# Attention with one query, forward and backward: transposes as fp32 blocks, and sums in four column groups

## The chip, the core and the metric

The kernel runs on one core of a Trainium2 chip. A core has a matrix engine (TensorE, PE in the profile; its weight loads have a row of their own, PEld), a vector engine (VectorE, DVE), a scalar engine (ScalarE, ACT), GpSimd (POOL), and SyncE (SP), which here only issues transfers. 16 DMA engines move data between the main memory (HBM) and the core's memory (SBUF); TensorE writes to PSUM, which VectorE and ScalarE read. The metric is the device time in microseconds of one execution.

## The reference

For each of 64 heads (batch 2, 32 heads) there is one query row q of 128 elements, k and v of 8192 x 128, and a gradient g of 128 elements; all are bf16.

```python
scores = jnp.einsum("bhqd,bhkd->bhqk", q, k) * scale      # scale = 128 ** -0.5
p = softmax(scores)
out = jnp.einsum("bhqk,bhkd->bhqd", p, v)
_out, _vjp = jax.vjp(_f, q, k, v)
_grads = _vjp(grad_out)
return (_out, *_grads)
```

With dp = v g and dS = p (dp - sum(p dp)), the outputs are o = p v, dq = scale dS k, dk = scale dS q (an outer product of 8192 x 128) and dv = p g (another). Per head k and v are read (2 MB each) and dk and dv are written (2 MB each): 8 MB a head, 537 MB in all.

## The kernel before, in words

**Tiles.** k or v of one head is one SBUF tile of 128 partitions x 64 rows x 128 elements (2 MB); partition p holds rows 64p to 64p+63. There are 12 such tiles (NTILE), for six heads. dk and dv are made in place of k and v (`outer`, L427), stored from there, and the tile is loaded anew with k or v of the head six later (`load`, L100, with `slot_of`). Loads are issued by SP, stores by POOL (L445, or L89 in two parts); the last head's stores go in eight parts by SP. A load of a tile waits for the store of what lies in it. A head has four chunks (NCH) of 16 rows a partition (CH) for k and four for v.

**Split stores.** dk of the heads in SPREAD (4, 11, ..., 53: eight heads) is stored by `by_rows` (L89) as two transfers of 126 and of 2 partitions.

**One step.** The loop over g runs one chunk a step, eight steps a head; what later stages of earlier heads have to do is done in the same step. All instructions are kept in program order on each engine (`pin`). In a step PE does, in this order:

- `broadcast` (L178, in two of the steps): q or g of the head into all partitions, as a matmul of a broadcast column with the identity; VectorE copies it to qb (L187).
- `transpose_chunk` (L194): 16 transposes of 128x128 bf16 into the PSUM tile tp (two of these), which ScalarE copies to ev (L196, 128x2048, two of these).
- `join` (L409), the last sum over partitions of dq or o.
- `acc` (L372): four matmuls that sum 16 rows of a chunk of v (or k) by E_pad (or dS_pad). The weights are CW = 64 columns of the padded row of probabilities, the moving operand 512 columns; they go to NG = 2 groups of 64 output partitions. Of the 64 output rows in a group only four hold sums that are wanted; `pick` (L389, L395) takes them out with the mask `diag`.
- `spread_rows` (L228, in two of the steps): the scores lie in PSUM as rows (`raw`, copied to `rows` by VectorE, L221); four fp32 matmuls with the selector sel4 lay them over the partitions. An fp32 matmul is shown as two weight loads and two matmuls.
- `max_spread` (L251) and, on ScalarE, `expo` (L271); also `total` (L315) and, as an fp32 transpose, `max_all` (L244).
- `score_chunk` of the chunk before (L208): four matmuls over the 512 columns each of ev, into four groups of 32 output partitions. The weights are 32 columns of qdT that hold q (or g) in one column and zeros beside it; the chunk decides where the window on qdT begins, and so which row of `raw` the scores go to.

`outer` for head i comes in the steps 9 to 12 (dv) and 13 to 16 (dk) after the head's first. VectorE does `outer`, `pick`, the copies out of PSUM and the small steps of the softmax.

Of the kernel before, what the change touches and what calls it, by code (L numbers as in the profile page):

```python
# [9 lines left out]
ALU = mybir.AluOpType  # L10
AX = mybir.AxisListType
BF16 = mybir.dt.bfloat16
F32 = mybir.dt.float32

CH = 16
QT = 4
CW = 64
NG = 2
SG = 4
SW = 32  # L20
NTILE = 12
FIRST = 6
SPREAD = range(4, 60, 7)


@with_exitstack
def kernel(
# [11 lines left out]
    nc = tc.nc  # L39
    B, H, Sq, D = q.shape  # L40
    Sk = k.shape[2]
    P = nc.NUM_PARTITIONS
    assert Sq == 1 and D == P
    BH = B * H
# [3 lines left out]
    NCH = NT // CH  # L48
# [71 lines left out]
        load(j, 0)  # L120
        load(j, 1)

    ident_bf = const.tile([P, P], BF16)
    masks.make_identity(nc, ident_bf[:])
    ident_f = const.tile([P, P], F32)
    masks.make_identity(nc, ident_f[:])
    ones = const.tile([P, 1], F32)
    nc.vector.memset(ones[:], 1.0)
    groups = [g * P // NG for g in range(NG)]
# [8 lines left out]
    nc.vector.memset(E_pad[:], 0.0)  # L138
    nc.vector.memset(dS_pad[:], 0.0)

    sel4 = const.tile([P, NCH, SG], F32)
    nc.vector.memset(sel4[:], 0.0)
    for g in range(SG):
        nc.vector.tensor_copy(
            out=sel4[g * SW : (g + 1) * SW, :, g],
            in_=ident_f[g * SW : (g + 1) * SW, g * SW : g * SW + NCH],
        )

    Q0 = NCH - 1
    qdT = const.tile([P, 2, Q0 + NCH * BH + SW], BF16)  # L150
    nc.vector.memset(qdT[:], 0.0)
    for w in range(2):
        tps = ps_m.tile([P, BH], BF16, tag=f"acc{w}", name="tps")
        nc.tensor.transpose(tps[:], qd_nat[:BH, w, :], ident_bf[:BH, :BH])
        nc.vector.tensor_copy(
            out=qdT[:, w, Q0 : Q0 + NCH * BH].rearrange("p (i f) -> p i f", f=NCH)[:, :, 0],
            in_=tps[:],
        )

    dqT = const.tile([P, BH], BF16)  # L160
    oT = const.tile([P, BH], BF16)
# [1 line left out]
    def begin(i):  # L163
# [7 lines left out]
        h.lsum = sw[:, 2 * NT + 2 * P : 2 * NT + 2 * P + 2]  # L171
        h.mb = sw[:, 2 * NT + 2 * P + 2 : 2 * NT + 2 * P + 3]

    def broadcast(i, w):

        h = heads[i]
        pin(
            nc.tensor.matmul(  # L178
                h.qbp,
                lhsT=qdT[:, w, Q0 + NCH * i : Q0 + NCH * i + 1].to_broadcast([P, P]),  # L180
                rhs=ident_bf[:],
                start=True,
                stop=True,
            )
        )
        h.qb[w] = small.tile([P, D], BF16, tag=f"qb{w}", name="qb")
        pin(nc.vector.tensor_copy(out=h.qb[w][:], in_=h.qbp))  # L187

    def transpose_chunk(i, c):
        w, c = divmod(c, NCH)  # L190
        src = heads[i].tile[w]
        tp = ps_tp.tile([P, CH, P], BF16, tag="tp", name="tp")
        for t in range(CH):
            pin(nc.tensor.transpose(tp[:, t, :], src[:, c * CH + t, :], ident_bf[:]))  # L194
        ev = evp.tile([P, CH, P], BF16, tag="ev", name="ev")
        pin(nc.scalar.copy(out=ev[:], in_=tp[:]))  # L196
        return ev

    def score_chunk(i, c, ev):

        h = heads[i]
        w, c = divmod(c, NCH)
        if c == 0:
            h.raw = ps_sdp.tile([P, QT * P], F32, tag="raw", name="raw")
        q0 = Q0 + NCH * i - c
        for g in range(SG):
            pin(
                nc.tensor.matmul(  # L208
                    h.raw[g * SW : (g + 1) * SW, :],
                    lhsT=qdT[:, w, q0 : q0 + SW],  # L210
                    rhs=ev[:, g * QT : (g + 1) * QT, :].rearrange("p n d -> p (n d)"),
                    start=(c == 0),
                    stop=(c == NCH - 1),
                )
            )
# [7 lines left out]
    def spread_rows(i, w):  # L223

        h = heads[i]
        for t in range(QT):
            pin(
                nc.tensor.matmul(  # L228
                    h.score[w].rearrange("p (n t) -> p n t", t=QT)[:, :, t],
                    lhsT=h.rows[:, t * P : (t + 1) * P],  # L230
                    rhs=sel4[:].rearrange("p c g -> p (c g)"),
                    start=True,
                    stop=True,
                )
            )

    def max_part(i):
        h = heads[i]
        h.mp = small.tile([P, 1], F32, tag="mp", name="mp")
        pin(nc.vector.reduce_max(out=h.mp[:], in_=h.s, axis=AX.X))  # L240

    def max_all(i):
        h = heads[i]
        pin(nc.tensor.transpose(h.mT, h.mp[:], ident_f[:]))  # L244
        h.gm = small.tile([1, 1], F32, tag="gm", name="gm")
        pin(nc.vector.reduce_max(out=h.gm[:], in_=h.mT, axis=AX.X))  # L246

    def max_spread(i):
        h = heads[i]
        pin(  # L250
            nc.tensor.matmul(  # L251
                h.mb,
                lhsT=ones[0:1, :].to_broadcast([1, P]),
                rhs=h.gm[:],
                start=True,
                stop=True,
            )
        )
        h.negm = small.tile([P, 1], F32, tag="negm", name="negm")
        pin(  # L260
            nc.vector.tensor_scalar(
                out=h.negm[:], in0=h.mb, scalar1=-scale, scalar2=None, op0=ALU.mult
            )
        )

    def expo(i):
        h = heads[i]
        h.E_f = work.tile([P, NT], F32, tag="E_f", name="E_f")
        h.ld = small.tile([P, 2], F32, tag="ld", name="ld")
        pin(  # L270
            nc.scalar.activation(  # L271
                out=h.E_f[:],
                in_=h.s,
                func=ACT.Exp,
                bias=h.negm[:],
                scale=scale,
                accum_out=h.ld[:, 0:1],
            )
        )
        pin(nc.vector.tensor_copy(out=E_pad[:, 0:NT], in_=h.E_f[:]))  # L280
# [39 lines left out]
    def normalise_p(i):  # L320
        h = heads[i]
        total(h.lsum[:, 0:1], h.ld[:, 0:1])
        h.rl = small.tile([P, 1], F32, tag="rl", name="rl")
        pin(nc.vector.reciprocal(out=h.rl[:], in_=h.lsum[:, 0:1]))
        pairs(i, 1, h.E_f, h.rl[:], "p2")
        h.rls = small.tile([P, 1], F32, tag="rls", name="rls")
        pin(
            nc.vector.tensor_scalar(
                out=h.rls[:], in0=h.rl[:], scalar1=scale, scalar2=None, op0=ALU.mult
            )  # L330
        )

    def normalise_ds(i):
        h = heads[i]
        total(h.lsum[:, 1:2], h.ld[:, 1:2])
        negdelta = small.tile([P, 1], F32, tag="negdelta", name="negdelta")
        pin(
            nc.vector.tensor_scalar(
                out=negdelta[:],
                in0=h.lsum[:, 1:2],  # L340
                scalar1=h.rl[:],
                scalar2=-1.0,
                op0=ALU.mult,
                op1=ALU.mult,
            )
        )
        dSu = work.tile([P, NT], F32, tag="dSu", name="dSu")
        pin(
            nc.vector.scalar_tensor_tensor(
                out=dSu[:],  # L350
                in0=h.dp,
                scalar=negdelta[:],
                in1=h.E_f[:],
                op0=ALU.add,
                op1=ALU.mult,
            )
        )
        pin(nc.vector.tensor_copy(out=dS_pad[:, 0:NT], in_=dSu[:]))  # L358
        pairs(i, 0, dSu, h.rls[:], "ds2")

    def acc(i, w, c):

# [42 lines left out]
    def join(i, w):  # L405

        h = heads[i]
        pin(
            nc.tensor.matmul(h.acc[w][:, 0:1], lhsT=h.sel[:], rhs=ones[:], start=True, stop=True)  # L409
        )  # L410
        pin(
            nc.vector.tensor_scalar(
                out=(oT if w else dqT)[:, i : i + 1],
                in0=h.acc[w][:, 0:1],
                scalar1=(h.rl if w else h.rls)[:],
                scalar2=None,
                op0=ALU.mult,
            )
        )
# [32 lines left out]
    last = list(range(1, NCH + 1))  # L452
    AHEAD = NTILE // 2

    prev = None
    for g in range(SL * BH + O0 + NCH + 4 - SL):
        now = [(g // SL - b, g % SL + b * SL) for b in range(4)]
# [2 lines left out]
        def at(r0):  # L460

            return next((i for i, r in now if r == r0), None)
# [37 lines left out]
        if prev is not None:  # L500
            score_chunk(*prev)
        prev = (g // SL, g % SL, ev) if ev is not None else None

        if (i := at(NCH)) is not None:
            keep_raw(i)
# [16 lines left out]

    for w, (src, dst) in enumerate(((dqT, out_1), (oT, out_0))):
        tps = ps_m.tile([BH, P], BF16, tag=f"acc{w}", name="tps")
        nc.tensor.transpose(tps[:], src[:], ident_bf[:])
        nat = evp.tile([P, CH, P], BF16, tag="ev", name="nat")
        nc.vector.tensor_copy(out=nat[:BH, 0, :], in_=tps[:])
        load_eng.dma_start(out=dst.rearrange("b h s d -> (b h s) d"), in_=nat[:BH, 0, :])
# [30 lines left out]
```

## Time and profile before

| | |
|---|---|
| median of 3 runs | 1280.13 us (1279.72 to 1282.18) |
| profiled execution, first to last instruction | 1280.2 us |
| mean granted TensorE clock | 0.991 of full speed |
| HBM read / written | 268.47 MB / 268.47 MB |
| busy: PE / DVE / ACT / POOL | 1190.2 / 1025.8 / 975.3 / 76.0 us |
| L194 transposes, 8192 | 544.4 us, 220 ns each from start to end of one |
| L196 evacuations of transposes, 512 | 954.5 us, 1865 ns each |
| L208 scores, 2048 | 205.2 us, 391 ns each |
| L372 sums, 2 x 1024 | 160.2 and 159.8 us, 393 ns each |
| DMA: queue 1 (loads, and the last stores) / queue 0 (stores) / queue 8 (instructions) | 50.1% / 49.0% / 0.5% of 16 engines' span |

The page's first part gives each engine's busy time and its share of the span. Its second part cuts the span into 40 slices and gives the busy tenths in each, also of the DMA engines. A group's busy time counts overlapping instructions once, so 8192 transposes of 220 ns take 544.4 us: they run one into the other. The timeline gives, for each run of like instructions, its start, its length, engine, line, operation, what is written and read, and in brackets the idle time before it with the one that ended it. A line on windows gives, for a stretch of the span, the busy time of PE, PEld, DVE, ACT and POOL, the granted clock, the DMA share, and GB/s. The list of issues gives how long a transfer took from its issue until it had landed.

### The profile page before, as it was taken

The numbers are of one execution on the slowest core, as the hardware profiler recorded it, in microseconds if no ns is written. First come the engines' busy times: TensorE is split into PE (matmuls) and PEld (weight loads), VectorE is DVE, ScalarE is ACT, GpSimd is POOL, SyncE is SP. The second block draws the span as 40 slices with busy tenths as digits, with TensorE's granted clock in tenths as the row PEclk, the third lists the DMA queues.
The fourth block names the chain that finished last, engine by engine and source line by source line (L and its number), as shares of the span: only waits on it lengthen the run. The fifth ranks groups of instructions, "written<-read, shape, count | busy, mean of one in ns | idle before, by whom it ended". The sixth has DMA issues, their size and how long they took to land.

```text
span 1280.2 us, 32473 instructions
## 1 busy us (share of the span) xinstructions
PE 1190.2 (93%) x14148; PEld 810.6 (63%) x14148; DVE 1025.8 (80%) x2256; ACT 975.3 (76%) x641; POOL 76.0 (6%) x143
## 2 busy tenths in 40 slices
PE   6999999999999999999999999999999999999994
PEld 5666666666666666666666666666666666666662
DVE  2888887888877888888888878788778888888885
ACT  6777777778777777777777777787777777777771
POOL 0000000000000000000000000000000000000000
PEclk9999999999999999999999999999999999999996
DMA  9999999999999999999999999999999999999996
GB/s 392 423 428 428 428 427 429 430 426 429 427 430 425 414 427 429 428 423 428 428 429 419 425 428 426 427 421 427 427 423 421 427 429 428 420 425 428 428 411 273
DMA packets 40155, 539.03 MB, mean 421 GB/s; under 512 B 5196, under 2 KB 5196, under 8 KB 6476
## 3 DMA queue, kind: packets, MB, share of 16 engines
q1 hardware_dynamic: 20172, 272.70, 50.1%
q0 software_dynamic: 19840, 264.25, 49.0%
q8 instruction: 110, 1.80, 0.5%
q14 instruction: 33, 0.27, 0.1%
HBM read 268.47 MB, written 268.47 MB: 419 GB/s over the span
## 4 chain that ended last, share of the span: by engine, by line
PE 59%; DVE 16%; ACT 10%; issue 10%; DMA 4%; POOL 0%; SPq 0%; ACTq 0%; POOLq 0%; DVEq 0%
PE tp L194 24%; PE acc L372 15%; ACT ev L196 9%; PE raw L208 9%; DVE kvt L427 6%; PE sw L228 4%; DVE sel L395 4%; DMA out_dram<-kvt 3%; DVE rows L221 3%; PE sw L315 3%; PE sw L178 2%; PE acc L409 2%; ACT E_f L271 1%; DVE sel L389 1%; DVE E_pad L280 1%
## 5 line engine op out<-in xcount | busy, mean ns | idle before, releaser
L196 ACT COPY ev<-tp 128x2048 bf16<-128x2048 bf16 x512 | 954.5, 1865 | 275.6 <-PE tp L194 268.9
L427 DVE TENSOR_TENSOR kvt<-qb,pair 128x2048 bf16<-128x2048 bf16 x512 | 616.8, 1216 | 0.2
L194 PE MATMUL tp<-ident_bf,kvt 128*128 128x128 bf16 x8192 | 544.4, 220 | 0.0
L194 PEld LDWEIGHTS <-kvt 128*128 128x128 bf16 x8192 | 482.4, 99 | 81.6 <-issue 80.7
L208 PE MATMUL raw<-ev,qdT 128*32 128x512 bf16 x2048 | 205.2, 391 | 1.5 <-ACT ev L196 1.5
L372 PE MATMUL acc<-kvt,E_pad 128*64 128x512 bf16 x1024 | 160.2, 393 | 24.5 <-DVE E_pad L280 24.5
L372 PE MATMUL acc<-kvt,dS_pad 128*64 128x512 bf16 x1024 | 159.8, 393 | 0.1
L228 PEld LDWEIGHTS sw<-sel,rows 128*128 128x128 f32 x1024 | 124.7, 192 | 52.4 <-DVE sel L395 25.9
L395 DVE SCALAR_TENSOR_TENSOR sel<-acc,diag,sel 128x128 f32<-128x128 f32 x384 | 134.8, 351 | 13.6
L208 PEld LDWEIGHTS <-qdT 128*32 128x32 bf16 x2048 | 53.1, 93 | 136.6 <-issue 131.8
L228 PE MATMUL sw<-sel,rows 128*128 128x16 f32 x1024 | 137.1, 266 | 0.0
L445 POOL DMA_DIRECT2D out_dram<-kvt x118 | 63.3, 536 | 1094.0 <-DVE kvt L427 555.7
L221 DVE COPY rows<-raw 128x512 f32<-128x512 f32 x128 | 88.6, 692 | 22.4 <-PE raw L208 22.4
L280 DVE CAST E_pad<-E_f 128x64 bf16<-128x64 f32 x64 | 12.5, 195 | 80.3 <-ACT E_f L271 80.3
L372 PEld LDWEIGHTS <-E_pad 128*64 128x64 bf16 x1024 | 36.1, 108 | 49.9 <-DVE E_pad L280 35.7
L178 PE MATMUL sw<-ident_bf,qdT 128*128 128x128 bf16 x128 | 28.5, 223 | 38.2 <-DVE mp L240 38.2
L246 DVE TENSOR_REDUCE gm<-sw 1x1 f32<-1x128 f32 x64 | 17.9, 279 | 55.4 <-PE sw L244 55.4
L315 PEld LDWEIGHTS sw<-ld,ones 128*128 128x128 f32 x256 | 38.1, 188 | 29.7 <-issue 15.0
L372 PEld LDWEIGHTS <-dS_pad 128*64 128x64 bf16 x1024 | 36.4, 108 | 22.3 <-DVE dS_pad L358 1.0
L315 PE MATMUL sw<-ld,ones 128*128 128x1 f32 x256 | 49.1, 261 | 0.0
L409 PE MATMUL acc<-ones,sel 128*128 128x1 f32 x256 | 43.3, 239 | 5.3 <-DVE sel L395 5.3
L389 DVE TENSOR_SCALAR sel<-acc,diag 128x128 f32<-128x128 f32 x128 | 43.8, 342 | 0.0
(49 smaller groups left out, 377.1 us busy)
## 6 DMA issues: line engine op xcount, KB each, us to landing
out_dram<-kvt POOLq DMA_DIRECT2D x118, 2048.0 KB, 40.6
kvt<-in_v_dram SPq DMA_DIRECT2D x64, 2048.0 KB, 19.1
kvt<-in_k_dram SPq DMA_DIRECT2D x63, 2048.0 KB, 19.4
out_dram<-kvt POOLq DMA_DIRECT2D x8, 2016.0 KB, 44.9
out_dram<-kvt SPq DMA_DIRECT2D x8, 512.0 KB, 10.9
kvt<-in_k_dram SPq DMA_DIRECT2D x2, 512.0 KB, 4.3
kvt<-in_k_dram SPq DMA_DIRECT2D x1, 1024.0 KB, 6.9
out_dram<-kvt POOLq DMA_DIRECT2D x8, 32.0 KB, 44.3
```

What stands on the lines that cost most here:

```text
L194: pin(nc.tensor.transpose(tp[:, t, :], src[:, c * CH + t, :], ident_bf[:]))
L196: pin(nc.scalar.copy(out=ev[:], in_=tp[:]))
L208: nc.tensor.matmul(h.raw[g * SW : (g + 1) * SW, :], lhsT=qdT[:, w, q0 : q0 + SW], rhs=ev[:, g * QT : (g + 1) * QT, :].rearrange("p n d -> ...
L221: pin(nc.vector.tensor_copy(out=h.rows[:], in_=h.raw[:]))
L228: nc.tensor.matmul(h.score[w].rearrange("p (n t) -> p n t", t=QT)[:, :, t], lhsT=h.rows[:, t * P : (t + 1) * P], rhs=sel4[:].rearrange("p ...
L315: nc.tensor.matmul(out, lhsT=ones[:].to_broadcast([P, P]), rhs=col, start=True, stop=True)
L372: nc.tensor.matmul(h.acc[w][g : g + CW, :], lhsT=wts[:, n0 : n0 + CW], rhs=rows[:, n0 : n0 + QT, :].rearrange("p n d -> p (n d)"), start=( ...
L389: nc.vector.tensor_scalar(out=h.sel[:], in0=block, scalar1=diag[:, 0:1], scalar2=None, op0=ALU.mult)
L395: nc.vector.scalar_tensor_tensor(out=h.sel[:], in0=block, scalar=diag[:, b : b + 1], in1=h.sel[:], op0=ALU.mult, op1=ALU.add,)
L409: nc.tensor.matmul(h.acc[w][:, 0:1], lhsT=h.sel[:], rhs=ones[:], start=True, stop=True)
L427: nc.vector.tensor_tensor(out=h.tile[w][:, n0 : n0 + CH, :].rearrange("p n (e t) -> p n e t", t=2), in0=h.qb[w][:] .rearrange("p (e t) -> ...
L445: pin(eng.dma_start(out=dst[:, b0:b1, :], in_=h.tile[w][:, b0:b1, :]))
```

## The change

- **Transposes.** Two neighbouring rows of a partition, 2 x 128 bf16, are taken as 128 fp32 words, and the 128x128 block of words is transposed as fp32. A chunk has 8 such transposes in place of 16. tp and ev are fp32 tiles of 128x1024 (as many bytes as before). A word of ev holds two neighbouring elements e = 0, 1 of one row; its partition tells the row's parity t and the pair of elements.
- **Scores.** `score_chunk` reads ev as bf16 with a step of two elements, once with the even and once with the odd elements. Its weights are a window on `qwin`, which holds two columns for one head, one for each parity. `window`, a ScalarE copy of 128x2x2 out of `qpair`, fills it for the next head; it is called twice a head. `qpair` is made once, by four more transposes and VectorE copies. qdT is replaced by qT, qpair and qwin.
- **The selector.** sel4 has pairs of columns, so that `spread_rows` writes pairs of neighbouring columns.
- **Identity.** ident_bf is no longer made: it is the upper half of each word of ident_f, read with a step of two.
- **Sums.** CW = 32 and NG = 4: the four matmuls of `acc` have 32 weight columns each and go to four groups of 32 output partitions.
- **Split stores.** SPREAD is 6, 18, 30, 42, 54: five heads.
- **Small tiles.** mp, gm, negm, ld, rl, rls and negdelta of a head become columns of one tile `st`.

The core of the diff (the renaming of the small tiles is left out):

```diff
-CW = 64
-NG = 2
+CW = 32
+NG = 4
...
-SPREAD = range(4, 60, 7)
+SPREAD = range(6, 60, 12)
...
-    ident_bf = const.tile([P, P], BF16)
-    masks.make_identity(nc, ident_bf[:])
     ident_f = const.tile([P, P], F32)
     masks.make_identity(nc, ident_f[:])
+    ident_bf = ident_f[:].bitcast(BF16).rearrange("p (n e) -> p n e", e=2)[:, :, 1]
...
-    Q0 = NCH - 1
-    qdT = const.tile([P, 2, Q0 + NCH * BH + SW], BF16)
-    nc.vector.memset(qdT[:], 0.0)
+    Q0 = 2 * NCH - 2
+    qT = const.tile([P, 2, BH], BF16)
+    qpair = const.tile([P, 2, BH, 2, 2], BF16)
+    nc.vector.memset(qpair[:], 0.0)
+    qwin = const.tile([P, 2, 2, Q0 + SW], BF16)
+    nc.vector.memset(qwin[:], 0.0)
+    qd_pair = evp.tile([P, 2, 2, 2, D // 2], BF16, tag="ev", name="qd_pair")
+    for w in range(2):
+        nc.vector.tensor_copy(
+            out=qd_pair[:BH, w],
+            in_=qd_nat[:BH, w, :]
+            .rearrange("p (j e) -> p e j", e=2)
+            .unsqueeze(2)
+            .to_broadcast([BH, 2, 2, D // 2]),
+        )
+        for e in range(2):
+            tps = ps_m.tile([P, BH], BF16, tag=f"acc{e}", name="tps")
+            nc.tensor.transpose(
+                tps[:],
+                qd_pair[:BH, w, e].rearrange("p t j -> p (t j)"),
+                ident_bf[:BH, :BH],
+            )
+            for t in range(2):
+                half = slice(t * D // 2, (t + 1) * D // 2)
+                nc.vector.tensor_copy(out=qpair[half, w, :, e, t], in_=tps[half, :])
...
+    def window(i, w):
+
+        pin(nc.scalar.copy(out=qwin[:, w, :, Q0 : Q0 + 2], in_=qpair[:, w, i]))
+
...
-        tp = ps_tp.tile([P, CH, P], BF16, tag="tp", name="tp")
-        for t in range(CH):
-            pin(nc.tensor.transpose(tp[:, t, :], src[:, c * CH + t, :], ident_bf[:]))
-        ev = evp.tile([P, CH, P], BF16, tag="ev", name="ev")
+        tp = ps_tp.tile([P, CH // 2, P], F32, tag="tp", name="tp")
+        for m in range(CH // 2):
+            n0 = c * CH + 2 * m
+            two = src[:, n0 : n0 + 2, :].rearrange("p n d -> p (n d)").bitcast(F32)
+            pin(nc.tensor.transpose(tp[:, m, :], two, ident_f[:]))
+        ev = evp.tile([P, CH // 2, P], F32, tag="ev", name="ev")
         pin(nc.scalar.copy(out=ev[:], in_=tp[:]))
...
-        q0 = Q0 + NCH * i - c
+        q0 = Q0 - 2 * c
+        cols = (
+            ev[:]
+            .rearrange("p m s -> p (m s)")
+            .bitcast(BF16)
+            .rearrange("p (b s e) -> p b s e", b=SG // 2, e=2)
+        )
         for g in range(SG):
+            b, e = divmod(g, 2)
             pin(
                 nc.tensor.matmul(
                     h.raw[g * SW : (g + 1) * SW, :],
-                    lhsT=qdT[:, w, q0 : q0 + SW],
-                    rhs=ev[:, g * QT : (g + 1) * QT, :].rearrange("p n d -> p (n d)"),
+                    lhsT=qwin[:, w, e, q0 : q0 + SW],
+                    rhs=cols[:, b, :, e],
                     start=(c == 0),
                     stop=(c == NCH - 1),
                 )
             )
...
-        for t in range(QT):
+        for m in range(QT):
             pin(
                 nc.tensor.matmul(
-                    h.score[w].rearrange("p (n t) -> p n t", t=QT)[:, :, t],
-                    lhsT=h.rows[:, t * P : (t + 1) * P],
-                    rhs=sel4[:].rearrange("p c g -> p (c g)"),
+                    h.score[w].rearrange("p (n m t) -> p n m t", m=QT, t=2)[:, :, m, :],
+                    lhsT=h.rows[:, m * P : (m + 1) * P],
+                    rhs=sel4[:].rearrange("p c b t -> p (c b t)"),
...
+    window(0, 0)
+    window(0, 1)
...
+        if (i := at(NCH + 1)) is not None and i + 1 < BH:
+            window(i + 1, 0)
+        if (i := at(1)) is not None and i > 0:
+            window(i, 1)
```

After the change the lines have other numbers: transposes L220 (evacuation L222), scores L241, `spread_rows` L261, `acc` L401, `outer` L456, stores L474.

More of the change, by code (lines that the diff above doesn't have):

```diff
@@ L139 @@
     nc.vector.memset(dS_pad[:], 0.0)
-    sel4 = const.tile([P, NCH, SG], F32)
+    sel4 = const.tile([P, NCH, SG // 2, 2], F32)
     nc.vector.memset(sel4[:], 0.0)
@@ L144 @@
         nc.vector.tensor_copy(
-            out=sel4[g * SW : (g + 1) * SW, :, g],
-            in_=ident_f[g * SW : (g + 1) * SW, g * SW : g * SW + NCH],
-        )
-    Q0 = NCH - 1
-    qdT = const.tile([P, 2, Q0 + NCH * BH + SW], BF16)
-    nc.vector.memset(qdT[:], 0.0)
+            out=sel4[g * SW : (g + 1) * SW, :, g // 2, :],
+            in_=ident_f[g * SW : (g + 1) * SW, g * SW : g * SW + 2 * NCH].rearrange(
+                "p (c t) -> p c t", t=2
+            ),
+        )
+    Q0 = 2 * NCH - 2
[23 more added lines that the diff above has]
+                nc.vector.tensor_copy(out=qpair[half, w, :, e, t], in_=tps[half, :])
     for w in range(2):
@@ L154 @@
         nc.tensor.transpose(tps[:], qd_nat[:BH, w, :], ident_bf[:BH, :BH])
[L155 to L158, printed above, removed]
+        nc.vector.tensor_copy(out=qT[:, w, :], in_=tps[:])
     dqT = const.tile([P, BH], BF16)
@@ L179, in broadcast @@
                 h.qbp,
-                lhsT=qdT[:, w, Q0 + NCH * i : Q0 + NCH * i + 1].to_broadcast([P, P]),
-                rhs=ident_bf[:],
+                lhsT=qT[:, w, i : i + 1].to_broadcast([P, P]),
+                rhs=ident_bf,
                 start=True,
@@ L238, in max_part @@
         h = heads[i]
-        h.mp = small.tile([P, 1], F32, tag="mp", name="mp")
-        pin(nc.vector.reduce_max(out=h.mp[:], in_=h.s, axis=AX.X))
+        st = small.tile([P, 8], F32, tag="st", name="st")
+        h.mp, h.gm, h.negm = st[:, 0:1], st[0:1, 1:2], st[:, 2:3]
+        h.ld, h.rl, h.rls, h.negdelta = st[:, 3:5], st[:, 5:6], st[:, 6:7], st[:, 7:8]
+        pin(nc.vector.reduce_max(out=h.mp, in_=h.s, axis=AX.X))
     def max_all(i):
         h = heads[i]
-        pin(nc.tensor.transpose(h.mT, h.mp[:], ident_f[:]))
-        h.gm = small.tile([1, 1], F32, tag="gm", name="gm")
-        pin(nc.vector.reduce_max(out=h.gm[:], in_=h.mT, axis=AX.X))
+        pin(nc.tensor.transpose(h.mT, h.mp, ident_f[:]))
+        pin(nc.vector.reduce_max(out=h.gm, in_=h.mT, axis=AX.X))
     def max_spread(i):
@@ L253, in max_spread @@
                 lhsT=ones[0:1, :].to_broadcast([1, P]),
-                rhs=h.gm[:],
+                rhs=h.gm,
                 start=True,
@@ L258, in max_spread @@
         )
-        h.negm = small.tile([P, 1], F32, tag="negm", name="negm")
         pin(
             nc.vector.tensor_scalar(
-                out=h.negm[:], in0=h.mb, scalar1=-scale, scalar2=None, op0=ALU.mult
+                out=h.negm, in0=h.mb, scalar1=-scale, scalar2=None, op0=ALU.mult
             )
@@ L268, in expo @@
         h.E_f = work.tile([P, NT], F32, tag="E_f", name="E_f")
-        h.ld = small.tile([P, 2], F32, tag="ld", name="ld")
         pin(
@@ L274, in expo @@
                 func=ACT.Exp,
-                bias=h.negm[:],
+                bias=h.negm,
                 scale=scale,
@@ L322, in normalise_p @@
         total(h.lsum[:, 0:1], h.ld[:, 0:1])
[L323 to L326, printed above, removed]
+        pin(nc.vector.reciprocal(out=h.rl, in_=h.lsum[:, 0:1]))
+        pairs(i, 1, h.E_f, h.rl, "p2")
         pin(
             nc.vector.tensor_scalar(
-                out=h.rls[:], in0=h.rl[:], scalar1=scale, scalar2=None, op0=ALU.mult
+                out=h.rls, in0=h.rl, scalar1=scale, scalar2=None, op0=ALU.mult
             )
@@ L335, in normalise_ds @@
         total(h.lsum[:, 1:2], h.ld[:, 1:2])
-        negdelta = small.tile([P, 1], F32, tag="negdelta", name="negdelta")
         pin(
             nc.vector.tensor_scalar(
-                out=negdelta[:],
+                out=h.negdelta,
                 in0=h.lsum[:, 1:2],
-                scalar1=h.rl[:],
+                scalar1=h.rl,
                 scalar2=-1.0,
@@ L351, in normalise_ds @@
                 in0=h.dp,
-                scalar=negdelta[:],
+                scalar=h.negdelta,
                 in1=h.E_f[:],
@@ L358, in normalise_ds @@
         pin(nc.vector.tensor_copy(out=dS_pad[:, 0:NT], in_=dSu[:]))
-        pairs(i, 0, dSu, h.rls[:], "ds2")
+        pairs(i, 0, dSu, h.rls, "ds2")
     def acc(i, w, c):
@@ L414, in join @@
                 in0=h.acc[w][:, 0:1],
-                scalar1=(h.rl if w else h.rls)[:],
+                scalar1=h.rl if w else h.rls,
                 scalar2=None,
@@ L524 @@
         tps = ps_m.tile([BH, P], BF16, tag=f"acc{w}", name="tps")
-        nc.tensor.transpose(tps[:], src[:], ident_bf[:])
+        nc.tensor.transpose(tps[:], src[:], ident_bf)
         nat = evp.tile([P, CH, P], BF16, tag="ev", name="nat")
```

## The prediction

> **What bounds the kernel now.** I read the page first, sections 1 and 2 (engines, then the 40 slices with the DMA row), then the windows, then the groups, the timeline of PE, and the landing of loads against PE's first use of them. Two things look full at once:
>
> ```profile
> PE 1190.2 (93%) x14148; PEld 810.6 (63%) x14148; DVE 1025.8 (80%) x2256; ACT 975.3 (76%) x641; POOL 76.0 (6%) x143
> ...
> PE   6999999999999999999999999999999999999994
> ...
> DMA  9999999999999999999999999999999999999996
> ```
>
> To tell which of the two sets the pace, look for who waits. PE's waits name DVE and ACT, never a load after the start. The head period is read from the one L244 that each head has: 19.445 us from start to start, the same all through (64 of them are 1244.5 us of the 1280.2). The loads are ahead of PE. The last k tile:
>
> ```profile
> 1201.70 0.33 SPq L100 DMA_DIRECT2D kvt<-in_k_dram  x1
> ...
> kvt<-in_k_dram SPq DMA_DIRECT2D x1, 2048.0 KB, 18.6
> ...
> 1231.11 1.07 PE L194 MATMUL tp<-ident_bf,kvt 128*128 128x128 bf16 x16
> ```
>
> Issued at 1201.7, landed 18.6 us later at 1220.3, first transposed at 1231.1: the tile lay ready for 10.8 us. The same difference is 34.7 us at head 20, 26.2 at head 32, 17.6 at head 48. So **PE's own program is the bound**, and DMA is close behind and slower: it eats the lead that the 12 tiles loaded in advance gave. Whatever PE saves, only these 10.8 us can be had before the loads are the bound. The DMA has no room of its own:
>
> ```profile
> 20.00:1230.00 1210.00, 1149.33 (x13755) 783.41 (x13753) 988.84 (x2168) 948.27 (x623) 72.58 (x131) 1.00 1.01 426
> 1230.00:1255.00 25.00, 22.67 (x251) 14.91 (x251) 19.84 (x46) 17.40 (x13) 1.59 (x3) 0.98 0.84 355
> 1255.00:1270.00 15.00, 8.20 (x38) 3.92 (x37) 13.65 (x27) 0.00 (x0) 0.00 (x0) 0.61 0.99 411
> 1270.00:1281.00 11.00, 0.01 (x1) 0.00 (x0) 0.35 (x2) 0.00 (x0) 0.00 (x0) 0.50 0.21 83
> ```
>
> The last two columns are the DMA share and GB/s: 1.01 and 426 GB/s from 20 to 1230 us, 0.84 between 1230 and 1255, when the loads are over and stores come at PE's pace. The profiled execution's span, 1280.2 us, is the median of the runs (1280.13), so the sums below need no shift.
>
> **The change, part by part, in PE time of one head.** These rows carry it:
>
> ```profile
> 612.40 0.62 PE L372 MATMUL acc<-kvt,E_pad 128*64 128x512 bf16 x4
> 612.95 1.06 PE L228 MATMUL sw<-sel,rows 128*128 128x16 f32 x8
> 613.95 0.40 PE L208 MATMUL raw<-ev,qdT 128*32 128x512 bf16 x4
> ...
> 606.58 0.27 PE L244 MATMUL sw<-ident_f,mp 128*1 128x128 f32 x1
> 606.69 1.05 PE L194 MATMUL tp<-ident_bf,kvt 128*128 128x128 bf16 x16
> ```
>
> Bursts are priced from start to start of the next, since a matmul's end includes its drain.
>
> 1. *Sums for dq and o.* A burst of four at 64 columns takes 0.553 us (median). With 32 columns in four groups it has the form of L208, four matmuls of 512 columns in four groups, which takes 0.332. Eight bursts a head: 8 x (0.332 - 0.553) = **-1.77 us**. The bursts of L372 and L208 then share one form; where one follows the other a change of form may go, some 0.09 us each, which I leave out of the sum.
>
> 2. *Transposes.* 128 at 0.056 us (start to start) become 64 in fp32. A price for one has two sides. The stream: L244 is an fp32 transpose, one pass over 128 columns, and the next matmul starts 0.108 us after it. The weights: the fp32 loads of L228 follow one another at 0.111 us. The bf16 transposes show the next load starting 2 ns after the matmul before has started, so loads lie under the stream, and the bf16 load behind L244 did too. If fp32 loads do the same, one takes the larger, 0.111; if not, the sum, 0.219; the low end is 0.108. 64 x 0.108 to 64 x 0.219 is 6.9 to 14.0 us against 128 x 0.056 = 7.17: from -0.3 to +6.9 us. I take 0.111, that is **-0.07 us**, because L409's fp32 load starts 1 ns after the last bf16 transpose has started and so lies under a stream as well.
>
> 3. *Scores.* The moving operand now takes every second bf16 of ev, 4 bytes a step. No row of this trace moves strided columns. Free is one end, 0.332 a burst. The other is the ratio of L244 to L194, where 4 bytes a column cost 0.108 against 0.056: 512 columns at half rate add 0.236 (the spacing of two rounds in L372), 8 x 0.236 = +1.89 us a head. Below nothing there is no reason. I take 0: the fp32 rate need not come from bytes read. ident_bf is strided as well: two broadcasts a head, 0 to 0.10 us.
>
> The Trainium skill (Advanced Engine Details and Errata, SBUF Cachelines) says that SBUF reads keep full speed while at least two accesses fall into a 16-byte line; four of these do, so by it part 3 costs 0 and not 1.89. No row here shows it.
>
> 4. *ACT.* 512 evacuations of 128x2048 bf16 at 1.865 us become 128x1024 fp32: between half of that (0.93) and all of it. 128 window copies are added, between 0.20 (the accumulator read) and 0.32 us (E_f). ACT goes from 15.2 to 8-16 us a head. It lies beside PE; a window copy waits for nothing that is late, and only the next evacuation is queued behind it. If it had no cover it would cost 0.6 us a head. Taken: 0.
>
> 5. *Set-up.* Ten DVE copies at 0.17 to 0.31 us and four transposes come ahead of the first transpose of k (9.08 us). PE starts some 4 us later. Loads cover it (the lead at head 2 is 15 us); if PE stayed the bound, all 4 us would be paid.
>
> 6. *L228, pick, the joined small tile.* L228 has the same eight passes, which go by the weight loads, and the same waits. 0.
>
> 7. *DMA.* Instruction fetches are 1.80 MB in 110 packets (queue 8). The programs built have 28,868 and 16,724 instructions, so 1.80 x (1 - 0.58) = 0.76 MB goes: at 426 GB/s **-1.8 us** of DMA time. Five split dk stores in place of eight move no bytes less; each shifts at most an eighth of a 2 MB store (4.9 us) between engines, so three shift +-1.8 us; taken as 0.
>
> PE's head: 19.445 - 1.77 - 0.07 = 17.6 us. PE needs to fall only to 19.445 - 10.8/63.5 = 19.27 to meet the last load, so **the loads become the bound** and most of PE's gain goes into waiting for them.
>
> The end then comes from the bytes: 539.03 - 0.76 = 538.27 MB. The first 20 us move 20 x 0.371 = 7.4 MB as before; 530.85 MB at 426 GB/s take 1246.1 us, so the queue is empty at 1266. The last output's issue to the end took 9.9 us (1270.29 to 1280.2), with a queue in front of it; the small q load landed in 5.7, so I take 5. Sum **1271 us**. From the other side, compute: 1280.2 - 10.8 - 1.8 = 1267.6, which the bytes overrule. What is late next is the DMA.
>
> The Trainium skill (DMA: Bandwidth & Descriptors, Specifications) gives 435 GB/s as the ceiling of the 16 engines, a rule against hoping for more; this trace's 426 is 98% of it. By 435 the 530.85 MB take 1220.3 us and the estimate would be 1245.
>
> **Rivals.**
> - *fp32 weight loads don't lie under the fp32 stream.* Then a transpose is 0.219: PE's head is 17.6 + 64 x 0.108 = 24.5 us, and 64 x 24.5 + 35.7 (what the span has beside 64 periods) + 4 = **1608 us**. It decides from 0.137 us a transpose (64 x 0.026 = 1.67, up to 19.27). For it: no row pairs the two. Against it: both halves of the pair lie under other streams.
> - *The strided read runs at half rate.* 17.6 + 1.89 + 0.10 = 19.6 a head: 64 x 0.15 + 4 = +14, **1294 us**. Slower from 0.55 us a score burst; below about 0.53 the loads are the bound anyway. With the changes of form of part 1 saved (six bursts, 0.5 us) it ends near 1272.
> - *The gain is hidden by uneven DMA engines.* Between 1230 and 1255 the share is 0.84 with stores outstanding: some engines are dry, others not. If the late ones set the end, bytes per core don't count and the end stays, less the fetches: **1278 us**.
>
> **How the numbers follow.** Loads bound, 1264 to 1276: 0.62. Uneven engines, 1276 to 1282: 0.12. Half rate: 0.13, about half of it at 1283 to 1296, the rest faster or level. Serial weight loads: 0.08. A wait that I did not see, either way: 0.05. A measurement of this kernel can tell about 0.2% (2.6 us) from no change. Faster: 0.62 + 0.05 of half rate + 0.03 = 0.70; within 0.2%: 0.12; slower: 0.18. The range runs from 1262, the bytes with 1.8 us more from the split stores and the last output landing at once, to 1288, into the half-rate case; the serial loads and the worst half-rate are outside.
>
> **What would show it.** Right: starts of L220 0.111 us apart; bursts of L401 at 0.33; PE waiting for loads of kvt, its lead gone before head 40; ACT near 60 to 65% busy or less; DMA share 1.0 up to about 1260; queue 8 near 1.04 MB. Wrong: L220 starts above 0.137 apart; score bursts of 0.5 or more; the lead of the loads still there at the last head; or the share falling well below 1 before the loads end.

## The result and the profile after

The median is **1272.3 us** (1271.48 to 1272.72) against 1281.16 us for the kernel before, run beside it: a ratio of 0.9932 with a 95% interval of 0.9913 to 0.9951. The profiled execution spans 1269.7 us (before: 1280.2). A run's time is 1.8 us more than its span (1271.48 us for the one profiled), so the span before belongs to an execution of about 1282 us, the slowest of its three: the two spans differ by 10.5 us, the medians by 8.9. The forecast was 1271 us.

First the page of the changed kernel: engines, PE and DMA in 40 slices, and the instruction fetches.

```profile
PE 1073.2 (85%) x10056; PEld 757.9 (60%) x10056; DVE 1020.8 (80%) x2269; ACT 552.0 (43%) x769; POOL 72.9 (6%) x138
...
PE   6999999999888997988897888888888889898870
...
DMA  9999999999999999999999999999999999999997
...
q8 instruction: 79, 1.29, 0.4%
```

PE is no longer full: its digit falls to 8 after the first quarter. ACT has lost 423 us of work. The DMA row is full up to the last slice, as before. The fetches went from 110 packets and 1.80 MB to 79 and 1.29 MB.

Who waits now, from the list of waits of the changed kernel (total us, times, longest):

```profile
DVE E_pad L312 <- ACT E_f L303: 38.9, 64, 0.9
...
PE tp L220 <- DMA kvt<-in_v_dram: 70.5, 38, 6.0
...
PE tp L220 <- DMA kvt<-in_k_dram: 25.4, 30, 1.8
```

VectorE waits 38.9 us for ScalarE's part of the softmax, where it waited 80.3 before. PE waits for loads, 96 us in all, which it never did before. The loads' lead over PE's first use is 13.5 us at head 8, 1.7 at head 16, 0.1 at head 20, and stays between 0 and 4 us after that.

The bursts of PE, from its timeline in the middle of the span (start, duration, line, count):

```profile
605.89 0.40 PE L401 MATMUL acc<-kvt,dS_pad 128*32 128x512 bf16 x4
606.12 0.40 PE L241 MATMUL raw<-ev,qwin 128*32 128x512 bf16 x4
606.45 1.09 PE L220 MATMUL tp<-ident_f,kvt 128*128 128x128 f32 x8
607.47 0.40 PE L401 MATMUL acc<-kvt,dS_pad 128*32 128x512 bf16 x4
607.80 1.06 PE L261 MATMUL sw<-sel,rows 128*128 128x16 f32 x8
608.80 0.41 PE L241 MATMUL raw<-ev,qwin 128*32 128x512 bf16 x4
```

A burst of sums takes 0.33 us where an fp32 form follows (607.47 to 607.80) and 0.23 where the scores follow, which have its own form (605.89 to 606.12). A score burst with its step of two takes 0.33 (606.12 to 606.45), as it did before. Eight fp32 transposes take 1.00 us up to the next burst (median), 0.109 us from one to the next. Where PE waits for no load its head takes 17.30 us.

The stretches of the span (busy us of PE, PEld, DVE, ACT, POOL with counts, then clock, DMA share, GB/s):

```profile
20.00:1230.00 1210.00, 1057.68 (x9963) 747.76 (x9960) 1000.28 (x2208) 546.76 (x763) 71.16 (x131) 0.97 1.01 428
1230.00:1255.00 25.00, 6.76 (x42) 3.52 (x42) 15.30 (x35) 0.00 (x0) 0.33 (x1) 0.55 0.97 410
1255.00:1270.00 15.00, 0.00 (x0) 0.00 (x0) 0.00 (x0) 0.00 (x0) 0.00 (x0) 0.50 0.41 167
```

The last compute ends at 1247, where it ended at 1270 before. After that only stores run, and not on all engines: from 1255 to 1270 the DMA share is 0.41, six or seven of sixteen engines in the mean, with transfers outstanding nearly to the end. That is the first sign that the sixteen DMA engines do not end together.

### The profile page after: what moved, and what is told of

Read it like the earlier page. It is cut to its first block, busy times and chain, and to the rows that moved or that the text cites. A ratio compares the mean times of both kernels' runs of the same rounds, so it can differ in the third digit from the quotient of the medians.

```text
span 1269.7 us, 24553 instructions
## 1 busy us (share of the span) xinstructions
PE 1073.2 (85%) x10056; PEld 757.9 (60%) x10056; DVE 1020.8 (80%) x2269; ACT 552.0 (43%) x769; POOL 72.9 (6%) x138
## 2 busy tenths in 40 slices
DMA packets 39501, 538.53 MB, mean 424 GB/s; under 512 B 4956, under 2 KB 4956, under 8 KB 6236
## 3 DMA queue, kind: packets, MB, share of 16 engines
q8 instruction: 79, 1.29, 0.4%
## 4 chain that ended last, share of the span: by engine, by line
DMA 33%; another core or an unknown queue 22%; DVE 17%; PE 13%; issue 9%; ACT 2%; SPq 1%; POOL 1%; ACTq 0%; POOLq 0%; DVEq 0%
DMA kvt<-in_v_dram 18%; DMA kvt<-in_k_dram 10%; DVE kvt L456 9%; PE tp L220 8%; DMA out_dram<-kvt 4%; DVE sel L424 3%; DVE rows L254 2%; PE acc L401 2%; PE raw L241 2%; ACT ev L222 1%; SPq L100 1%; DVE sel L418 1%; PE sw L261 1%; DVE pair L335 1%
## 5 line engine op out<-in xcount | busy, mean ns | idle before, releaser
L222 ACT COPY ev<-tp 128x1024 f32<-128x1024 f32 x512 | 518.6, 1013 | 665.5 <-PE tp L220 659.3
L220 PE MATMUL tp<-ident_f,kvt 128*128 128x128 f32 x4096 | 566.2, 283 | 96.0 <-DMA kvt<-in_v_dram 70.5
L456 DVE TENSOR_TENSOR kvt<-qb,pair 128x2048 bf16<-128x2048 bf16 x512 | 616.9, 1216 | 0.1
L220 PEld LDWEIGHTS tp<-ident_f,kvt 128*128 128x128 f32 x4096 | 470.2, 147 | 216.5 <-issue 170.6
L241 PE MATMUL raw<-ev,qwin 128*32 128x512 bf16 x2048 | 210.3, 400 | 0.0
L261 PEld LDWEIGHTS sw<-sel,rows 128*128 128x128 f32 x1024 | 125.5, 193 | 30.4 <-DVE sel L418 15.2
L261 PE MATMUL sw<-sel,rows 128*128 128x16 f32 x1024 | 138.0, 267 | 0.5 <-DVE st L355 0.5
L474 POOL DMA_DIRECT2D out_dram<-kvt x121 | 64.7, 534 | 1106.3 <-DVE kvt L456 507.3
L401 PE MATMUL acc<-kvt,dS_pad 128*32 128x512 bf16 x1024 | 107.3, 410 | 0.8 <-DVE dS_pad L387 0.8
L401 PE MATMUL acc<-kvt,E_pad 128*32 128x512 bf16 x1024 | 103.0, 392 | 0.7 <-DVE E_pad L312 0.7
L202 PE MATMUL sw<-ident_f,qT 128*128 128x128 bf16 x128 | 29.1, 227 | 55.3 <-DVE st L275 55.1
L347 PEld LDWEIGHTS sw<-st,ones 128*128 128x128 f32 x256 | 38.4, 189 | 56.2 <-issue 54.5
L241 PEld LDWEIGHTS <-qwin 128*32 128x32 bf16 x2048 | 54.0, 95 | 5.4 <-issue 1.0
L347 PE MATMUL sw<-st,ones 128*128 128x1 f32 x256 | 49.3, 262 | 0.5 <-DVE st L318 0.5
L401 PEld LDWEIGHTS <-dS_pad 128*32 128x32 bf16 x1024 | 26.4, 94 | 36.2 <-issue 29.1
L401 PEld LDWEIGHTS <-E_pad 128*32 128x32 bf16 x1024 | 26.3, 93 | 33.7 <-issue 28.8
L438 PEld LDWEIGHTS acc<-ones,sel 128*128 128x128 f32 x256 | 39.8, 197 | 8.1 <-DVE sel L424 8.1
L312 DVE CAST E_pad<-E_f 128x64 bf16<-128x64 f32 x64 | 12.5, 195 | 38.9 <-ACT E_f L303 38.9
## 6 DMA issues: line engine op xcount, KB each, us to landing
kvt<-in_v_dram SPq DMA_DIRECT2D x64, 2048.0 KB, 20.1
out_dram<-kvt POOLq DMA_DIRECT2D x5, 2016.0 KB, 71.2
```

The source lines that it names most:

```text
L220: pin(nc.tensor.transpose(tp[:, m, :], two, ident_f[:]))
L241: nc.tensor.matmul(h.raw[g * SW : (g + 1) * SW, :], lhsT=qwin[:, w, e, q0 : q0 + SW], rhs=cols[:, b, :, e], start=(c == 0), stop=(c == NCH ...
L261: nc.tensor.matmul(h.score[w].rearrange("p (n m t) -> p n m t", m=QT, t=2)[:, :, m, :], lhsT=h.rows[:, m * P : (m + 1) * P], rhs=sel4[:].r ...
L347: nc.tensor.matmul(out, lhsT=ones[:].to_broadcast([P, P]), rhs=col, start=True, stop=True)
L401: nc.tensor.matmul(h.acc[w][g : g + CW, :], lhsT=wts[:, n0 : n0 + CW], rhs=rows[:, n0 : n0 + QT, :].rearrange("p n d -> p (n d)"), start=( ...
L456: nc.vector.tensor_tensor(out=h.tile[w][:, n0 : n0 + CH, :].rearrange("p n (e t) -> p n e t", t=2), in0=h.qb[w][:] .rearrange("p (e t) -> ...
```

## The experiments

Three theories could explain a gain of 9 us:

- **P** (the prediction's): PE's saving moved the bound from PE to the loads; the end then follows from the bytes.
- **F**: instruction fetches load few DMA engines, so 0.51 MB less of them is worth far more than its bytes. Later runs ask the same of the split stores as a means against it.
- **S**: each split store costs DMA time and gives nothing back, so three fewer are a gain.

**1. The sums alone.** The kernel before with one edit:

```diff
-CW = 64
-NG = 2
+CW = 32
+NG = 4
```

> The kernel before with CW = 32 and NG = 4 alone. Theory (PE was the bound, the loads are next): a burst of sums falls from 0.553 to 0.33 us, and to 0.23 where a score burst follows, so PE's head falls by 1.8 to 2.3 us to 17.1 to 17.6, under the 19.3 at which PE meets the last load. The loads bind; instruction fetches stay at 1.80 MB, so the time is that of the changed kernel plus 1 to 2 us: 1272 to 1275. Rival (the transposes and the relief of ScalarE carry the gain): ScalarE stays at 15.2 us a head with 1.865 us a chunk and holds the steps up; PE's head stays near 19 and the time at 1277 to 1281.

Measured: 1282.08 us, ratio 1.0004 (0.9988 to 1.002). No gain: the time lies above both ranges. The rival was right about PE, whose head is 19.14 us (median) where the theory had 17.1 to 17.6. The span is 1278.5. From its list of waits:

```profile
PE tp L194 <- DMA kvt<-in_v_dram: 23.9, 12, 3.9
...
PE tp L194 <- DMA kvt<-in_k_dram: 6.3, 9, 1.1
```

The loads' lead is used up: the last v tile is transposed first at 1228.3 us (before: 1240.8), and from head 48 on PE waits for loads. The last output is issued at 1258.1 (before: 1270.3). All that P needs for its gain has happened, and the end has not moved. In the tail the engines dry up one after another; the DMA share of this kernel in steps of 5 us from 1255:

```profile
1255.00:1260.00 5.00, 0.90 (x3) 0.63 (x3) 2.00 (x8) 0.00 (x0) 0.00 (x0) 0.50 0.92 384
1260.00:1265.00 5.00, 0.00 (x0) 0.00 (x0) 0.00 (x0) 0.00 (x0) 0.00 (x0) 0.50 0.58 243
1265.00:1270.00 5.00, 0.00 (x0) 0.00 (x0) 0.00 (x0) 0.00 (x0) 0.00 (x0) 0.50 0.50 208
1270.00:1275.00 5.00, 0.00 (x0) 0.00 (x0) 0.00 (x0) 0.00 (x0) 0.00 (x0) 0.50 0.35 139
```

Compute is over before 1260, yet 0.58 to 0.35 of the DMA capacity, some nine and then six engines of sixteen, works on from there to 1275. The late engines set the end, not the sum of the bytes.

**2. The rest of the change without the sums.** The changed kernel with its sums put back, and with its five split stores:

```diff
-CW = 32
-NG = 4
+CW = 64
+NG = 2
```

> The changed kernel with CW = 64 and NG = 2: transposes, strided scores, windows and five split stores, without the sums. Theory: PE's head is that of the changed kernel, 17.3, plus 1.8 to 2.3 us for the bursts of sums, 19.1 to 19.6, on both sides of the 19.3 that matters: 1273 to 1285, with PE's lead over the loads small but seldom gone. Rival (the transposes carry the gain): 1272, and PE waits for loads from head 16 on as in the changed kernel.

Measured: 1272.12 us, ratio 0.9928 (0.99 to 0.9956): the whole gain, with PE at 94% of the span, a head of 19.01 us, and 2.0 us of waits of PE for loads. That is the rival's time with the theory's lead: the loads catch up with PE only near head 56. The sums are worth nothing here.

**3. and 4. More work for PE.** The changed kernel with the transposes of two, then of four of a head's eight chunks done twice (the second time into the same place):

```diff
-        for m in range(CH // 2):
+        for r in range(2 if (w, c) in ((0, 1), (1, 1)) else 1):
+            for m in range(CH // 2):
```

> The changed kernel with the transposes of two chunks a head made twice: 16 more fp32 transposes, 16 x 0.109 = 1.75 us more PE work a head, 112 us in all. Theory: PE's head rises from 17.3 to 19.05, still under the loads' pace, so the time stays within 3 us of the changed kernel's 1272. Rival (PE's work still ends last, less of it gives less time): 1272 + 112 = 1384.

> The same with four chunks a head: 3.5 us more a head, PE's head 20.8. Theory: PE is the bound again, 64 x 20.8 + 33 = 1364 us, with no wait for a load after the start. Rival (the loads go on to bind, PE's work is hidden): 1272 to 1280.

Measured: 1272.43 us, 0.9929 (0.9905 to 0.9953), with two chunks, and 1287.16 us, 1.0044 (1.0031 to 1.0057), with four. Two more chunks put 85 us on PE's busy time and nothing on the end. Four make PE the bound: busy 98%, no wait for loads, 19.56 us a head all through. The size expected there was too high: 16 more transposes a head added 0.69 us to PE's head (17.30 to 17.99) and not 1.75, because part of them fell into PE's wait for VectorE's softmax (L202 waits for `st`, 55.1 us in all in the changed kernel and 4.5 with two chunks more); the next 16 added 1.57. The runs bracket the price of PE: at 17.99 us a head, and at the 19.01 of run 2, it costs nothing, at 19.56 it sets the time. In run 4 the end comes 3.8 us after the issue of the last outputs (span 1285.7):

```profile
1281.91 1.14 SPq L564 DMA_DIRECT2D out_dram<-nat  x2
```

**5. and 6. Five split stores in the kernels that keep 1.80 MB of fetches.** The kernel before, and run 1, each with

```diff
-SPREAD = range(4, 60, 7)
+SPREAD = range(6, 60, 12)
```

> The kernel before with the five split stores of the changed one (6, 18, 30, 42, 54) in place of eight, and nothing else. The sums alone made PE wait for loads and still gained nothing, so something on the DMA side ends last. Theory S (the three further split stores cost the DMA engines time, because they load the engines unevenly): steady rate up from 426 to 428 GB/s and the time falls to 1272 to 1277, held by PE's head of 19.445. Theory F (the 1.80 MB of instruction fetches cost it; 1.29 in the changed kernel): no change, 1280 to 1282, or slower, if the split stores make up for the fetches.

> The sums in four groups and five split stores, bf16 transposes as before: fetches stay at 1.80 MB. Theory S: 1272 to 1274, the whole gain. Theory F: 1280 to 1284, as with the sums alone.

Measured: 1276.8 us, 0.9958 (0.9935 to 0.9981), and 1276.89 us, 0.9958 (0.9936 to 0.9979). The same gain with a full PE and with one that waits for loads (19 us in all in run 6): 3.6 us against the kernel before run beside them (1280.4), some 40% of the change's. Run 5 lies in S's range and not in F's; run 6 lies between the two. How the end moves is plain in SP's timeline at the end, first of the kernel before, then of the kernel before with five:

```profile
1256.72 11.34 SPq L445 DMA_DIRECT2D out_dram<-kvt  x8
1270.29 1.88 SPq L528 DMA_DIRECT2D out_dram<-nat  x2
```

```profile
1255.95 11.19 SPq L445 DMA_DIRECT2D out_dram<-kvt  x8
1269.75 1.14 SPq L528 DMA_DIRECT2D out_dram<-nat  x2
```

The last outputs are issued at the same time, 0.5 us apart, so PE has done nothing for it. But the spans end at 1280.2 and 1274.4: what lies behind these issues shrank from 9.9 to 4.7 us (the profiled execution before was a slow one, so by some 2 us less in the medians). The backlog of late engines was there, and it was smaller.

Runs 5 and 6 end together by chance. Run 5's 4.7 us are nearly the 3.8 us of run 4, where PE sets the time: with five splits PE's 19.445 us a head are again the bound to within 1 us (from run 5 to run 4, 0.115 us more a head is 7.4 us and PE's first transpose is 4.4 us later, 11.8 in all; the spans differ by 11.3). And at 1.80 MB of fetches the DMA engines allow no less (run 6, whose last output is issued at 1253.9 and which ends at 1275.4). So the kernel before had two limits some 5 us apart, the late DMA engines and just under them PE. Relief of the DMA alone could not have gone below about 1276; the changed kernel needs some of PE's saving too, and the 19.01 us of run 2 are enough.

**7. Eight split stores in the changed kernel.**

```diff
-SPREAD = range(6, 60, 12)
+SPREAD = range(4, 60, 7)
```

> The changed kernel with the eight split stores of before; fetches 1.29 MB. Theory S: most of the gain is lost, 1278 to 1282. Theory F: 1272, nothing lost.

Measured: 1274.52 us, 0.995 (0.9926 to 0.9975), in neither range. Eight cost 2.2 us against five in the medians; that is near what these runs can tell, since the ten executions spread from 1272.5 to 1281.9 us, and nine of them lie above all four of the changed kernel. The 5.9 us that remain to the kernel before (1280.4 beside this run) come with eight splits on both sides: they belong to what else was changed.

**8. More fetches, first try.** The changed kernel with 56 matmuls of one column a head that write an unused column:

```diff
+            if r >= NCH:
+                for _ in range(14):
+                    pin(
+                        nc.tensor.matmul(
+                            heads[i].junk,
+                            lhsT=qT[:, 0, 0:32],
+                            rhs=qT[:, 0, 0:1],
...
```

> The changed kernel with 56 matmuls of one column more a head (7168 more instructions with their weight loads, about 0.46 MB more of fetches, 1.75 in all, at some 1.7 us of PE a head, which 16 extra transposes showed to cost nothing). Their results go to a spare column and are not used. Theory S: 1272 to 1274. Theory F: 1279 to 1282.

Measured: 1363.03 us, 1.0634 (1.0557 to 1.0711), with 1.75 MB of fetches. It tells nothing of their price: PE's head grew to about 21 us, with 83 us of waits of the first of these matmuls for VectorE, so PE was the bound.

**9. More fetches, with PE's work unchanged.** The matmuls of scores and sums of chunks 1 to 3 as two of 256 columns in place of one of 512: 6144 instructions more, the same columns.

```diff
+        parts = 2 if c else 1
+        for s in range(parts):
...
-                    rhs=cols[:, b, :, e],
+                        rhs=cols[:, b, half, e],
```

> The changed kernel with the score and sum matmuls of the chunks 1 to 3 of a tile made as two of 256 columns in place of one of 512: 6144 more instructions, so fetches rise from 1.29 to about 1.68 MB, while the columns streamed, and so nearly PE's time, stay; five split stores as before. Theory F (fetches cost the DMA engines time; the transposes' gain of some 4.5 us at five split stores is their 0.51 MB): 0.39 of 0.51 MB come back, so 3 to 4 us, 1275 to 1276. Rival (something else of the transposes gives the gain, such as less work on ScalarE): 1272, unchanged.

Measured: 1275.57 us, 0.9954 (0.9936 to 0.9971), **3.3 us slower** than the changed kernel. From its page:

```profile
PE 1079.6 (85%) x13128; PEld 820.6 (64%) x13128; DVE 1021.9 (80%) x2269; ACT 552.6 (43%) x769; POOL 73.1 (6%) x138
...
q8 instruction: 103, 1.69, 0.5%
```

PE's busy time and its share are nearly what they were, a burst takes 0.23 or 0.33 us as before, a head without waits 17.30 us, and the fetches rose by 0.40 MB. At 428 GB/s that is 0.9 us; it cost 3.3 (all nine executions, from 1274.7 us, lie above those of the changed kernel, to 1272.7). F's number: scaled to 0.51 MB it is 4.2 of the 4.5 us that the changed kernel gains over run 5, which leaves 0.3 us for the rival. One run does not fit so well: run 3 fetched 1.43 MB, which at this price costs 1.2 us, and was 0.1 us slower.

**10. to 12. Fewer split stores.** The changed kernel with none and with two (`SPREAD = ()` and `(18, 42)`), and the kernel before with none:

```diff
-SPREAD = range(6, 60, 12)
+SPREAD = ()
```

> The changed kernel with no split stores. Theory S (each split store costs the engines that take a ninth row 0.6 us and gives nothing back): five fewer give 3 us, 1269. Rival (the split stores make up for the fetches, which lie on few engines): the engines with the fetches end later, 1275 or more, and loads land later in one or two of 16 shares.

> The changed kernel with two split stores (heads 18 and 42). Theory S: 1270.5, between five and none. Rival: between 1272 and the time with none, and so slower than five.

> The kernel before with no split stores; fetches 1.80 MB. Theory S: faster than with five, 1274 to 1276, as far as PE's head of 19.445 lets it. Rival: slower than with five, 1277 to 1290, since 1.80 MB of fetches have nothing that makes up for them.

Measured: 1283.21 us, 1.0016 (1.0003 to 1.0029); 1275.87 us, 0.9952 (0.9933 to 0.9971); 1294.71 us, 1.0105 (1.0081 to 1.0129). S falls, and the rival's direction holds in all three (the last one is 4.7 us beyond its range): without the splits both kernels are slower, by 10.9 us (five to none) and by 12.7 us (eight to none; 1282.0 beside this run). The mark of it is the landing of a load, from the list of DMA issues (count, KB, median us to landing); first the changed kernel, then with two, then with none:

```profile
kvt<-in_v_dram SPq DMA_DIRECT2D x64, 2048.0 KB, 20.1
```

```profile
kvt<-in_v_dram SPq DMA_DIRECT2D x64, 2048.0 KB, 29.7
```

```profile
kvt<-in_v_dram SPq DMA_DIRECT2D x64, 2048.0 KB, 44.8
```

The bytes are the same in all three. With no splits a load's last part lands 25 us later, since one part of every transfer queues on an engine that is behind: by the landing records of the traces the last of a load's sixteen parts comes 6.2 us (median) after the fifteenth, against 0.6 with five. In the kernel before with none a load takes 42.6 us, and the last part comes 8.7 us after the fifteenth. The end of the changed kernel with none shows the one engine alone, all compute being over by 1271.4:

```profile
1275.00:1280.00 5.00, 0.00 (x0) 0.00 (x0) 0.00 (x0) 0.00 (x0) 0.00 (x0) 0.50 0.06 26
```

A share of 0.06 is one engine of sixteen. With five or eight splits it is several that end late (0.41 in the changed kernel, 0.58 to 0.35 in run 1). A landing that grows while the rate stays at 428 GB/s is an engine falling behind.

All times together, in us:

| split stores | fetches 1.80 MB (before) | 1.29 MB (changed) | 1.69 MB (changed, halves) |
|---|---|---|---|
| 0 | 1294.7 | 1283.2 | |
| 2 | | 1275.9 | |
| 5 | 1276.8 | 1272.3 | 1275.6 |
| 8 | 1280.4 to 1282.0 | 1274.5 | |

Down a column the time falls by about 3.6 us a split store at first (1283.2 to 1275.9 with two) and rises at the end by 0.7 (changed, five to eight) or 1.2 (before). The kernel before, run beside three groups of these runs, had medians of 1281.9, 1280.4 and 1282.0 us, so a difference of under 2 us between groups tells little. Along a row the kernel with 0.51 MB less of fetches is faster by 11.5 us at none and 4.5 at five. At five run 9 shows that it is the fetches; at none the two kernels differ in PE's and ScalarE's work as well, and no run there changes the fetches alone. At 44 GB/s (0.51 MB in 11.5 us), against 428 / 16 = 26.8 GB/s for one engine, the fetches behave as if one or two engines carried them; by the row at five (0.51 MB in 4.5 us, 113 GB/s) it would be about four. That is an estimate from the times; the trace does not tell which engine carries a packet, and so it stays open which ones they are, and whether the fetches alone make the one engine late. Open too is what in a split store helps: the rows may go to other engines, and each split also adds 128 data packets at the same bytes (39,501 packets with five and 38,461 with none, of which 4,956 and 4,556 are under 512 B). And the heads at which the splits lie may matter beside their number, since both differ between these runs.

No version beat the changed kernel; runs 2 and 3 equal it.

## Why the prediction was right and wrong

**The number and the sign were right, and the reason given for them was not**, so that the number came within 1.3 us was luck. Step by step:

- *What bounds the kernel now: PE's program, then the 10.8 us of lead.* The views were read rightly, and the conclusion drawn from them failed. PE was close to being the bound, but was not it: the late DMA engines ended some 5 us behind it (9.9 us after the last output's issue, 3.8 where PE is the bound). Run 1 used up the lead and gained nothing; run 2 left PE at 19.01 us a head and had all the gain; run 5 gains 3.6 us with PE's program untouched. The lead of the loads says when the loads will hold PE up. It does not say that the end comes earlier, for after the last load the stores still have to leave, and the late DMA engines set that. The trace of before held the sign: 9.9 us behind the last issue, of which "a queue in front" took 5. The share of 0.84 between 1230 and 1255, which the prediction took as a sign for a rival, is none by itself: in run 4, where PE is the bound, it is 0.62 there.
- *Sums, -1.77 us a head.* The price was right: bursts of 0.33 in place of 0.553. The change of form that was left out is there too: 0.10 us less where L241 follows L401, five times a head. That would make 17.1 us of the 17.6; PE's head is 17.30, and the 0.2 us between were not traced. On the end the sums are worth nothing (run 1, and run 2 against the changed kernel).
- *Transposes, 0.111 us each.* Measured 0.109 from start to start, for the matmuls and for the weight loads alike: the fp32 weight load lies under the fp32 stream. The rival with serial loads (1608 us) is out.
- *Scores with a step of two, 0.* Measured 0.33 us a burst, as before: half rate (1294 us) is out. The Trainium skill (Advanced Engine Details and Errata, SBUF Cachelines) gave 0 for it and agrees with this row.
- *ACT, 0.* Its range held (43%), but it was not free of effect. In the kernel before PE waits 0.38 us a head for E_pad (24.5 us in 64 waits), and 0.6 for `mp`; in run 1 it waits 0.56 us for E_pad (31.9 in 57) and 1.15 for `mp` (71.2 in 62). That is part of why run 1's head was 19.14 us where the sums alone would give 17.7; the rest was not traced. With the shorter evacuations PE's wait for E_pad is gone (0.6 us in all in run 2). I take the cause to be the softmax step that is queued behind an evacuation on ScalarE; that was not tried by itself. In the changed kernel it is hidden behind the DMA in any case.
- *Set-up, some 4 us later, covered.* PE's first transpose of k starts at 12.3 us in place of 9.1, 3.2 us later. The loads' lead covers it.
- *DMA: fetches -1.8 us, split stores 0 (±1.8).* **This is the term that was mis-sized, and it is the whole gain, once PE is a little shorter.** Two things failed. The size of the fetches: 1.29 MB, not 1.04. The profile's counts (32,473 and 24,553) fall by 7,920, which at the 64 bytes of run 9 is 0.51 MB, what queue 8 lost; the built programs' counts fall by 12,144. The difference, 4,224, is nearly the 4,096 fp32 transposes, each of which the profile shows as a weight load and a matmul. And their price: they were priced at the rate of all engines, 0.51 MB = 1.2 us, where the runs show 4.5 us at five split stores (and, with more than the fetches changed, 11.5 at none). The split stores were taken as traffic moved between engines without a direction; they have one, which turns with their number: from none to five the changed kernel gains 10.9 us, and from eight to five it gains 2.2 and the kernel before 3.6.
- *The end from the bytes, 1271.* It met the time by two errors against each other. The rate was 428 and not 426 GB/s (some 6 us less over 1210 us), and the tail does not drain evenly (share 0.41 from 1255 on, where the sum had an empty queue at 1266 and 5 us more). A third is smaller: the sum gives a span, which is 1.8 us short of a run's time, and the prediction took no shift since the span of before happened to equal the median. By the Trainium skill's 435 GB/s (DMA: Bandwidth & Descriptors, Specifications) the sum was 1245; the trace's rate is 98% of that figure, and the uneven tail is what the figure cannot tell.
- *The rival "uneven DMA engines", 1278, at 0.12.* Its mechanism, late engines that set the end, is the one that the runs show. Its price was wrong for the same reason: it gave the fetches the mean rate, and the split stores nothing.

Of the signs named beforehand, the spacing of L220, the bursts of L401, the lost lead and ACT came as said; queue 8 and the share up to 1260 did not (1.29 MB; the share is 0.52 from 1258 to 1261). The signs that came were those of PE's prices and of the loads, which did not decide the time. Those that failed were on the DMA.

## What to carry to other kernels

When the DMA row is full, look at how the engines end and not only at how many bytes there are: a share well below 1 with transfers outstanding after the last compute, a stretch behind the last issue longer than where an engine is the bound (9.9 against 3.8 us here), or loads that land much later at an unchanged rate (44.8 against 20.1 us) say that some DMA engines are behind and set the time. Then count instructions as traffic (64 bytes each here), since a smaller program or a store split unevenly can be worth more than an engine's saving. And to show that an engine is the bound, give it more work and less: here 85 us more on PE, in the changed kernel, cost nothing, and the cheaper sums, in the kernel before, gained nothing. But ask for the next limit too: in the kernel before PE's own lay only some 5 us below that of the DMA engines.

## What the runs showed of the hardware

- Fetches: 6144 more instructions are 24 more packets and 0.40 MB on queue 8 (1.29 to 1.69 MB), so 64 bytes an instruction, and the time rose by 3.3 us. Two kernels of nearly the same DMA bytes (539.03 and 538.53 MB) differ by 11.5 us when no store is split, though not in the fetches alone.
- With no split store one of the sixteen engines falls behind and works on alone at the end (share 0.06 from 1275 to 1280). A store of 126 partitions with the last two stored apart is worth 3.6 us a store up to two; of the numbers tried, five is best for 1.29 MB of fetches.
- An fp32 transpose of 128x128 follows another after 0.109 us, twice the 0.056 of bf16, and carries two bf16 blocks; half as many cost PE the same and ScalarE 1.01 us in place of 1.87 for the evacuation.
- Four matmuls of 512 columns in four column groups take 0.33 us, and 0.23 when a burst of their own form follows, against 0.55 in two groups.
